# Storing half of three prepared operands out of seven, and rounding their high halves again when they are needed, in a fused attention and two-MoE kernel

## The chip, the cores and the metric

The kernel runs on one core of one Trainium2 chip. The metric is the device time of that core in microseconds; less is better. TensorE (PE) does the matrix products, VectorE (DVE), ScalarE (ACT) and GpSimd (POOL) the work between them, and SyncE (SP) issues every transfer. PEld is the load of weights into TensorE, DMA the sixteen transfer engines.

## The reference

Three layers follow each other on 2304 tokens:

```python
q_p, k_p = (phi(q_s), phi(k_s))          # random features, 32 heads
num = einsum(q_p, einsum(k_p, v)); den = einsum(q_p, sum(k_p))
x = (num / den), regrouped to [2304, 512]

logits = x @ w_gate                       # first MoE: 8 experts, all used
P = exp(logits - max); 8 times: P /= row sums, P /= column sums, P *= N/E
for e in range(8):
    h = maximum(x @ w1[e], 0)             # w1[e]: 512 x 1024
    out += P[:, e:e+1] * (h @ w2[e])      # w2[e]: 1024 x 512

h = maximum(maximum(x @ m1, x @ m2), x @ m3)   # second MoE, weights in float64
return h @ m_out
```

## The kernel before

Every operand of a product is split into a high part, rounded to the type that TensorE multiplies quickly, and a low part, the rest; a product is three matmuls (high by high, high by low, low by high: lines 406 to 408 and 808 to 810). The large products are done as seven products of half size instead of eight. For that the four blocks of a weight matrix are combined to seven operands, numbered 0 to 6: operands 0, 1 and 2 are blocks of the weight as it stands, 3 to 6 are sums and differences of blocks. A prepared operand is its high part and its low part side by side.

**Stages.** After attention (to about 145 us) the first MoE works on a third of the tokens at a time. *Stage 1* (about 145 to 690 us) takes the first third and runs through 32 slices of 256 hidden features, called subs. For each sub it loads w1 and w2 as they stand (512 KB each) into the tiles g, makes the sums on DVE or POOL, the high parts on ACT (L212) and the low parts on DVE or POOL (all those are recorded at L215), multiplies, and **stores all seven prepared operands** of w1 (`w1_store`) and of w2 (`prepare_w2`) in DRAM: 14 blocks of 128 KB for w1 and as many for w2, 1792 KB each. A sub is 42 matmuls of 384 columns and 36 of 512. *Phases 1 and 2* (about 690 to 1160 and to 1630 us) do the other two thirds: 16 units of two subs each, 168 matmuls of 384 columns a unit, and load the prepared operands instead of making them. w1's go into the one tile wa (256 KB a load, `before` in the loop over units), w2's into w2_0 to w2_6 (512 KB a load, in `second`). *Phases 3 to 5* are the second MoE, whose weights are prepared during phase 1 (`narrow`, `last_weights`) and loaded from lc1 and lc2.

**Order.** `Tasks` records each instruction with what it reads and writes and an estimated cost; `ordered` then plays a list schedule and writes out one fixed order for each engine. TensorE's own order is the program's; that of DVE, POOL, ACT and SP, and which of DVE and POOL takes a piece, follows from the costs, a transfer's bytes among them. Every engine then runs its list in order: an instruction that waits holds all behind it. `x_operands(1)` and `x_operands(2)` prepare the tokens of phases 1 and 2 (14 stores of 384 KB each, xc<-h) whenever the schedule has room in stage 1.

Of the kernel before, what the change touches and what calls it, by code (L numbers as in the profile page):

```python
# [8 lines left out]
F32 = mybir.dt.float32  # L9
# [145 lines left out]
def tile_performer__moe__max3(ctx, tc, kq_t, kq, v1, omega2, w_gate, w1, w2, m1, m2, m3, m_out, out):  # L155
# [7 lines left out]
    P = 128  # L163
# [60 lines left out]
    IN_B = {"w2_2", "w2_3", "w2_4", "w2_5", "w2_6", "b11", "b12", "b21", "b22", "t1", "t2", "t3", "t4", "pb", "ones"}  # L224
# [29 lines left out]
    def t_(k):  # L254
        return ts[k]
# [72 lines left out]
    def w1_store(s):  # L328
        dma(1792, lambda: wc1[s], lambda: ws[s % 2].bitcast(F32), all_w(s % 2), [("wc1", s)])
# [23 lines left out]
    def prepare_w2(s, late):  # L353
# [8 lines left out]
        for c, k in enumerate((h, l)):  # L362
            v = lambda k=k: t_(k).rearrange("p (k f) -> p k f", k=2).bitcast(F32)
            dma(256, lambda c=c: wc2[u][:, 0:2, c, sub], lambda v=v: v()[:, :, 0:256], [(k, 0), (k, 1)], [("wc2", u, sub, c)])
            dma(128, lambda c=c: wc2[u][:, 2, c, sub], lambda v=v: v()[:, 1, 256:], [(k, 1)], [("wc2", u, sub, 2 + c)])

        def rest():
# [5 lines left out]
            for c, k in enumerate(("w2_4", "w2_5")):  # L373
                dma(512, lambda c=c: wc2[u][:, 3:7, c, sub], lambda k=k: t_(k).rearrange("p (o f) -> p o f", o=4).bitcast(F32),
                    [(k, 0), (k, 1)], [("wc2", u, sub, 4 + c)])
# [128 lines left out]
    def retranspose(t):  # L504
# [7 lines left out]
        gi = g_next("st")  # L512
# [59 lines left out]
    def g_pieces():  # L572
        return [
            (lambda k=k, i=i: gs[k][:, i * 512 : i * 512 + Q], half(k, i)) for k in range(3) for i in range(2)
        ]
# [46 lines left out]
    def last_weights(item):  # L622
        n, m = item // 4, item % 4
        f0 = n * UF
        for at in range(2):
# [5 lines left out]
            narrow(lambda src=src: src, wide, at, 2, 3, at)  # L631
        if m < 3:
            add_all(left_operands(1, 3, 4, first_of(1)))
            dma(1792, lambda: lc1[3 * n + m], lambda: ws[1].bitcast(F32), all_w(1), [("lc1", 3 * n + m)])
        else:
# [4 lines left out]
            dma(1024, lambda: lc2[n].rearrange("p c f -> p (c f)"), lambda: flat()[:, 0:2048].bitcast(F32), ks[:8], [("lc2", n)])  # L640
# [40 lines left out]
    def program():  # L681
# [113 lines left out]
        def second(ph, u, j, d, n):  # L795
# [3 lines left out]
            if d == 0 and (ph == 1 or n):  # L799
                keys = [("wc2", u, sub, c) for sub in range(2) for c in range(6)]  # L800
# [559 lines left out]
```

## Time and profile before

| | us |
|---|---|
| median of 3 runs (lowest, highest) | 1948.44 (1946.2, 1950.5) |
| the profiled execution's own time | 1947.44 |
| span of its profile, first to last instruction | 1945.7 |

The page of the profile gives the busy share of each engine over the span: PE 97%, DVE 76%, POOL 52%, ACT 41%. 84.1% of the time of the sixteen DMA engines goes to the one queue that SP fills; 392.65 MB are read from DRAM and 177.26 MB written. The busy time of PE is modelled for pipelined matmuls, so the number of matmuls that a stretch completes tells more than its busy share. Such tables by stretch are called windows here.

### The profile page before, as it was taken

To read this page: it belongs to the slowest core of one execution; us is meant where nothing else is said; L and a number is where in the kernel's file an instruction comes from. 1 tells how busy PE (TensorE), PEld (TensorE's weight loads), DVE (VectorE), ACT (ScalarE), POOL (GpSimd) and SP (SyncE) were. 2 spreads that over 40 slices of the span, in tenths; PEclk is the share of its full clock that TensorE was granted. 3 is DMA by queue.
4 is the path that set the end of the run, shared out by engine and by line. 5 is a ranking of instruction groups with operands and counts; after the bars stand their busy time and mean duration, and the time that the engine had idled before them with its cause. 6 is when DMAs were issued, how large, how long until landed. Compare 5 with 4: busy or idle time off the path is not lost.

```text
span 1945.7 us, 33270 instructions
## 1 busy us (share of the span) xinstructions
PE 1881.6 (97%) x11521; PEld 1778.9 (91%) x11521; DVE 1482.3 (76%) x2676; ACT 796.9 (41%) x1805; POOL 1010.1 (52%) x933
## 2 busy tenths in 40 slices
PE   8997899899999999999999999999999999999998
PEld 6876788779999999999999998999999999989998
DVE  7874887778777766999989988999977767443435
ACT  7874345445444435333333333433433333232221
POOL 4532687335644416677777866677776444230000
PEclk9998999999999999999999999999999999999999
DMA  6655889979988899999898998988899889997673
GB/s 240 187 163 184 298 308 363 349 273 354 332 285 294 332 346 344 344 323 312 291 319 293 310 340 282 318 309 310 312 334 364 277 253 319 351 337 249 205 239 119
DMA packets 278759, 572.12 MB, mean 294 GB/s; under 512 B 26080, under 2 KB 125120, under 8 KB 272960
## 3 DMA queue, kind: packets, MB, share of 16 engines
q1 hardware_dynamic: 278592, 570.01, 84.1%
q8 instruction: 91, 1.49, 0.3%
q14 instruction: 76, 0.62, 0.1%
HBM read 392.65 MB, written 177.26 MB: 293 GB/s over the span
## 4 chain that ended last, share of the span: by engine, by line
PE 87%; DVE 6%; DMA 3%; ACT 2%; issue 1%; POOL 1%; SPq 0%; DVEq 0%; ACTq 0%
PE po L406 8%; PE po L408 8%; PE po L407 8%; PE ph L408 6%; PE ph L406 6%; PE ph L407 6%; PE ph L810 5%; PE ph L808 5%; PE ph L809 5%; PE ph L476 3%; PE ph L478 3%; PE ph L477 3%; PE small L810 3%; PE small L808 3%; PE small L809 3%; PE small L478 2%
## 5 line engine op out<-in xcount | busy, mean ns | idle before, releaser
L215 POOL TENSOR_TENSOR h<-b,h 128x384 fp32r<-128x384 f32 x149 | 164.6, 1112 | 177.5 <-ACT h L756 156.0
L406 PE MATMUL po<-x,wa 128*128 128x384 f32 x676 | 227.3, 336 | 4.0 <-DVE po L215 2.3
L407 PE MATMUL po<-x,wa 128*128 128x384 f32 x676 | 226.9, 336 | 0.0
L408 PE MATMUL po<-x,wa 128*128 128x384 f32 x676 | 226.8, 336 | 0.0
L406 PE MATMUL ph<-x,wa 128*128 128x384 f32 x588 | 199.6, 339 | 12.1 <-ACT wa L212 7.4
L408 PE MATMUL ph<-x,wa 128*128 128x384 f32 x588 | 199.7, 340 | 3.8 <-DVE wa L215 3.5
L810 PE MATMUL ph<-h,w 128*128 128x384 f32 x598 | 202.5, 339 | 0.0
L808 PE MATMUL ph<-h,w 128*128 128x384 f32 x598 | 202.3, 338 | 0.0
L809 PE MATMUL ph<-h,w 128*128 128x384 f32 x598 | 201.6, 337 | 0.0
L407 PE MATMUL ph<-x,wa 128*128 128x384 f32 x588 | 198.9, 338 | 0.0
L215 DVE TENSOR_TENSOR po<-po,u 128x384 f32<-128x384 f32 x230 | 129.0, 561 | 89.5 <-PE po L408 86.2
L215 DVE TENSOR_TENSOR acc<-ph,acc 128x384 f32<-128x384 f32 x280 | 154.0, 551 | 52.6 <-PE ph L810 51.6
L756 ACT CAST h<-b 128x384 fp32r<-128x384 f32 x192 | 98.8, 516 | 231.6 <-DVE b L771 207.5
L756 ACT CAST h<-t 128x384 fp32r<-128x384 f32 x256 | 129.2, 515 | 152.5 <-POOL t L215 104.0
L215 POOL TENSOR_TENSOR g<-g,g 128x256 f32<-128x256 f32 (+2 forms) x150 | 151.5, 1012 | 58.1 <-DVE g L617 23.3
L215 POOL TENSOR_TENSOR h<-t,h 128x384 fp32r<-128x384 f32 x126 | 137.4, 1091 | 85.0 <-ACT h L756 72.9
L413 ACT COPY u<-po 128x384 f32<-128x384 f32 x186 | 89.4, 482 | 182.1 <-PE po L408 178.6
L215 POOL TENSOR_TENSOR wb<-g,wb 128x512 fp32r<-128x512 f32 (+2 forms) x101 | 126.7, 1263 | 56.7 <-ACT wb L212 50.3
L413 ACT COPY u<-ph 128x384 f32<-128x384 f32 x183 | 88.0, 481 | 152.6 <-PE ph L408 151.2
L215 POOL TENSOR_TENSOR w<-g,w 128x512 fp32r<-128x512 f32 (+1 forms) x60 | 75.7, 1272 | 122.9 <-ACT w L212 50.7
L406 PEld LDWEIGHTS po<-x,wa 128*128 128x128 f32 x676 | 127.0, 188 | 6.8 <-DVE po L215 3.0
L476 PE MATMUL ph<-w,h 128*128 128x512 f32 x328 | 131.4, 401 | 0.0
(221 smaller groups left out, 5319.6 us busy)
## 6 DMA issues: line engine op xcount, KB each, us to landing
wa<-wc SPq DMA_DIRECT2D x441, 256.0 KB, 4.9
w<-wc SPq DMA_DIRECT2D x217, 512.0 KB, 5.5
g<-in_moe_w_dram SPq DMA_DIRECT2D x82, 512.0 KB, 6.1
wc<-w SPq DMA_DIRECT2D x64, 512.0 KB, 7.4
wc<-wa SPq DMA_DIRECT2D x16, 1792.0 KB, 9.0
wc<-wb SPq DMA_DIRECT2D x16, 1792.0 KB, 8.6
x<-xc SPq DMA_DIRECT2D x64, 384.0 KB, 7.4
wb<-lc SPq DMA_DIRECT2D x91, 256.0 KB, 4.6
```

Of the source, the lines that this page charges most:

```text
L215: (nc.gpsimd if on == "P" else nc.vector).tensor_tensor(out=out, in0=in0, in1=in1, op=op)
L406: nc.tensor.matmul(ps, w[:, 0, c], x[c][:, 0], start=c == 0 and not onto, stop=False, **given)
L407: nc.tensor.matmul(ps, w[:, 0, c], x[c][:, 1], start=False, stop=False, **given)
L408: nc.tensor.matmul(ps, w[:, 1, c], x[c][:, 0], start=False, stop=c == 1, **given)
L413: act(Q, lambda: nc.scalar.copy(t_(n), banks[b][:, :Q]), [b], [n])
L476: nc.tensor.matmul(ps, h[:, 0, c], t_(wh)[:, part], start=f == 0, stop=False)
L477: nc.tensor.matmul(ps, h[:, 0, c], t_(wl)[:, part], start=False, stop=False)
L478: nc.tensor.matmul(ps, h[:, 1, c], t_(wh)[:, part], start=False, stop=f == 1)
L756: act(Q, lambda: nc.scalar.copy(t_(h)[:, 0], t_(n)), [n], [(h, 0)])
L808: nc.tensor.matmul(ps, wv[:, 0, sub, d], h[:, 0], start=o == 0, stop=False)
L809: nc.tensor.matmul(ps, wv[:, 0, sub, d], h[:, 1], start=False, stop=False)
L810: nc.tensor.matmul(ps, wv[:, 1, sub, d], h[:, 0], start=False, stop=o == 1)
```

## The change

In stage 1 the high parts of operands 0, 1 and 2 are no longer stored. Their low parts go to new tensors wl1 and wl2, operands 3 to 6 go to wc1 and wc2 as before: 384 + 1024 KB a sub instead of 1792 KB, for w1 and for w2 alike. In phases 1 and 2 `load_w1` and `second` fetch the block of the weight itself for these three operands into one of six staging places of 128 KB (four quarters of g1, and the new tiles st0 and st1), and ACT rounds it into place (`round_high`); the low part is loaded beside it. The bytes loaded stay the same. A unit has 6 such operands of w1 (one raw load and one low load each) and 3 of w2 (two raw loads and one low load each): 33 transfers instead of 21, and 12 more copies of 256 columns on ACT. All prepared weights lie in DRAM as blocks, one operand behind the other, and no longer interleaved within a partition's row. Since g1 is the staging tile, the token copies after stage 1 use other g tiles, and `narrow` loads both of its pieces through g0.

```diff
-    wc1 = [dram.tile([P, 7, 2, 256], F32, name=f"wc1_{s}") for s in range(SUBS)]
-    wc2 = [dram.tile([P, 7, 2, 2, 256], F32, name=f"wc2_{u}") for u in range(UNITS)]
-    lc1 = [dram.tile([P, 7, 2, 256], F32, name=f"lc1_{a}") for a in range(9)]
-    lc2 = [dram.tile([P, 2, 1024], F32, name=f"lc2_{n}") for n in range(3)]
+    wl1 = [dram.tile([3, P, 256], F32, name=f"wl1_{s}") for s in range(SUBS)]
+    wc1 = [dram.tile([4, P, 2, 256], F32, name=f"wc1_{s}") for s in range(SUBS)]
+    wl2 = [dram.tile([3, P, 2, 256], F32, name=f"wl2_{u}") for u in range(UNITS)]
+    wc2 = [dram.tile([4, P, 2, 2, 256], F32, name=f"wc2_{u}") for u in range(UNITS)]
+    lc1 = [dram.tile([7, P, 2, 256], F32, name=f"lc1_{a}") for a in range(9)]
+    lc2 = [dram.tile([2, P, 1024], F32, name=f"lc2_{n}") for n in range(3)]
...
     def w1_store(s):
-        dma(1792, lambda: wc1[s], lambda: ws[s % 2].bitcast(F32), all_w(s % 2), [("wc1", s)])
+
+        kl, k = w_keys(s % 2, 0, 3)[1], w_keys(s % 2, 3, 7)
+        dma(384, lambda: wl1[s].rearrange("o p f -> p o f"), lambda: ws[s % 2][:, 0:3, 1].bitcast(F32), kl, [("wl1", s)])
+        dma(1024, lambda: wc1[s].rearrange("o p c f -> p o c f"), lambda: ws[s % 2][:, 3:7].bitcast(F32), k[0] + k[1], [("wc1", s)])
...
-        for c, k in enumerate((h, l)):
-            v = lambda k=k: t_(k).rearrange("p (k f) -> p k f", k=2).bitcast(F32)
-            dma(256, lambda c=c: wc2[u][:, 0:2, c, sub], lambda v=v: v()[:, :, 0:256], [(k, 0), (k, 1)], [("wc2", u, sub, c)])
-            dma(128, lambda c=c: wc2[u][:, 2, c, sub], lambda v=v: v()[:, 1, 256:], [(k, 1)], [("wc2", u, sub, 2 + c)])
+        v = lambda: t_(l).rearrange("p (k f) -> p k f", k=2).bitcast(F32)
+        dma(256, lambda: wl2[u][0:2, :, sub].rearrange("o p f -> p o f"), lambda: v()[:, :, 0:256], [(l, 0), (l, 1)], [("wl2", u, sub, 0)])
+        dma(128, lambda: wl2[u][2, :, sub], lambda: v()[:, 1, 256:], [(l, 1)], [("wl2", u, sub, 1)])
...
             if d == 0 and (ph == 1 or n):
-                keys = [("wc2", u, sub, c) for sub in range(2) for c in range(6)]
-                dma(512, lambda: t_(w).bitcast(F32), lambda: wc2[u][:, i].rearrange("p c s f -> p (c s f)"), keys, [(w, 0), (w, 1)])
+                keys = [("wl2" if i < 3 else "wc2", u, sub, c) for sub in range(2) for c in range(2)]
+                if i < 3:
+                    e, f0 = u // 2, u % 2 * 2 * UF
+                    for sub in range(2):
+                        high = lambda sub=sub: t_(w)[:, sub * 256 : (sub + 1) * 256]
+                        row = f0 + sub * UF + min(i, 1) * P
+                        round_high(high, lambda x: x, w2[e, row : row + P, slice(256, 512) if i == 2 else slice(0, 256)], [(w, 0)])
+                    dma(256, lambda: t_(w)[:, 512:].bitcast(F32), lambda: wl2[u][i].rearrange("p s f -> p (s f)"), keys, [(w, 1)])
+                else:
+                    dma(512, lambda: t_(w).bitcast(F32), lambda: wc2[u][i - 3].rearrange("p c s f -> p (c s f)"), keys, [(w, 0), (w, 1)])
...
+        stage = [(lambda q=q: gs[1][:, q * 256 : (q + 1) * 256], ("g1", q)) for q in range(4)]
+        stage += [(lambda k=k: t_(k), k) for k in ("st0", "st1")]
+
+        def round_high(out, shape, raw, keys):
+
+            stage.insert(0, stage.pop())
+            x, k = stage[0]
+            dma(128, lambda: shape(x()), lambda: raw, [], [k])
+            act(256, lambda: nc.scalar.copy(out(), x()), [k], keys)
+
+        def load_w1(s, i, kh, kl):
+            if i > 2:
+                dma(256, lambda: ws[0][:, i].bitcast(F32), lambda: wc1[s][i - 3], [("wc1", s)], kh + kl)
+                return
+            raw = w1_raw(s)[:, 2 * min(i, 1) : 2 * min(i, 1) + 2, P * (i // 2) : P * (i // 2 + 1)]
+            round_high(lambda: ws[0][:, i, 0], lambda x: x.rearrange("p (k f) -> p k f", k=2), raw, kh)
+            dma(128, lambda: ws[0][:, i, 1].bitcast(F32), lambda: wl1[s][i], [("wl1", s)], kl)
...
                         if ph == 1 or not first:
-                            dma(256, lambda: ws[0][:, i].bitcast(F32), lambda: wc1[s][:, i], [("wc1", s)], kh + kl)
+                            load_w1(s, i, kh, kl)
```

The first place that the prediction speaks of is SP's list in stage 1, from the store of sub 10's w1 operands on. Here wa and wb are the two tiles of prepared w1, w_0 to w_5 those of prepared w2, g the weights as loaded, b<-x_of and xc<-h the loads and stores of the tokens that x_operands prepares. Before:

```order
L218 DMA wc_10_106<-wa 128x3584
L218 DMA g_83<-in_moe_w_dram 128x2x512
L218 DMA b_2780<-x_of_87 128x384
L218 DMA xc_92<-h_2537 128x768
L218 DMA wc_5_133<-w_0_2535 128x2x256
L218 DMA wc_5_133<-w_0_2535 128x256
L218 DMA wc_5_133<-w_1_2536 128x2x256
L218 DMA wc_5_133<-w_1_2536 128x256
L218 DMA xc_92<-h_2541 128x768
L218 DMA xc_92<-h_2538 128x768
L218 DMA wc_4_132<-w_4_2776 128x4x256
```

Now:

```order
L220 DMA wl_10_106<-wa 128x3x256
L220 DMA g_83<-in_moe_w_dram 128x2x512
L220 DMA wc_4_180<-w_4_2823 128x4x256
L220 DMA wc_10_138<-wa 128x4x512
L220 DMA wc_4_180<-w_5_2824 128x4x256
L220 DMA wl_5_165<-w_1_2584 128x2x256
L220 DMA wl_5_165<-w_1_2584 128x256
L220 DMA wc_11_139<-wb 128x4x512
L220 DMA g_81<-in_moe_w_dram 128x4x256
L220 DMA wl_11_107<-wb 128x3x256
```

The stores of the high halves (w_0) are gone, and the token stores no longer stand here. Over the whole list, the 28 token stores xc<-h stood between the w1 stores of subs 1 and 13 before; now they stand between those of subs 1 and 21. Between the w1 stores of subs 5 and 16 there were 24, and there are 16.

The second place is SP's list in phase 1, where sub 17's weights are loaded (wa) and unit 8's (w_0, w_6, w_3). Before:

```order
L218 DMA w_2_2774<-wc_7_135 128x1024
L218 DMA wa<-wc_17_113 128x512 x2
L218 DMA w_0_2535<-wc_8_136 128x1024
L218 DMA wa<-wc_17_113 128x512 x2
L218 DMA w_6_2778<-wc_8_136 128x1024
L218 DMA wa<-wc_17_113 128x512 x2
L218 DMA w_3_2775<-wc_8_136 128x1024
L218 DMA wa<-wc_17_113 128x512
```

Now:

```order
L220 DMA w_2_2821<-wl_7_167 128x512
L220 DMA wa<-wl_17_113 128x256
L220 DMA g_82<-in_moe_w_dram 128x2x128
L220 DMA wa<-wc_17_145 128x512
L220 DMA g_82<-in_moe_w_dram 128x2x128
L220 DMA w_0_2583<-wl_8_168 128x512
L220 DMA g_82<-in_moe_w_dram 128x2x128
L220 DMA st_2838<-in_moe_w_dram 128x256
L220 DMA g_82<-in_moe_w_dram 128x256
L220 DMA wa<-wc_17_145 128x512
L220 DMA wa<-wl_17_113 128x256
```

The raw loads into the staging places (g_82 is g1, st) stand between the loads of the prepared weights.

The third place is ACT's list in the first half of a unit of phase 1, from the rounding of the first product of hidden features (h<-b) on. u are copies of products out of PSUM. Before:

```order
L756 CAST h_2537<-b_2779 128x384
L756 CAST h_2539<-b_2782 128x384
L756 CAST h_2540<-t_2783 128x384
L413 COPY u_2532<-po 128x384
L756 CAST h_2542<-t_2785 128x384
L413 COPY u_2533<-po 128x384
L413 COPY u_2534<-po 128x384
```

Now:

```order
L760 CAST h_2585<-b_2826 128x384
L760 CAST h_2587<-b_2829 128x384
L867 CAST wa<-g_82 128x256
L760 CAST h_2588<-t_2830 128x384
L417 COPY u_2580<-po 128x384
L867 CAST wa<-st_2839 128x256
L760 CAST h_2590<-t_2832 128x384
L417 COPY u_2581<-po 128x384
L417 COPY u_2582<-po 128x384
```

The roundings of the raw weights (L867) stand between the copies of PSUM and the casts of hidden features, and each waits for a raw load and for its place in wa or w.

## Rows read from the trace of the kernel before

**Rows 1.** The page, span and line 1 (busy, share, instructions of each engine).

```profile
span 1945.7 us, 33270 instructions
...
PE 1881.6 (97%) x11521; PEld 1778.9 (91%) x11521; DVE 1482.3 (76%) x2676; ACT 796.9 (41%) x1805; POOL 1010.1 (52%) x933
...
```

**Rows 2.** Windows: busy us (instructions) by engine, clock, DMA share, GB/s, by stage.

```profile
...
core 0: us, PE busy (x) PEld busy (x) DVE busy (x) ACT busy (x) POOL busy (x), PEclk, DMA share, GB/s
145.00:262.00 117.00, 93.58 (x517) 79.77 (x516) 86.73 (x177) 46.66 (x101) 61.80 (x62) 0.90 0.70 248
262.00:450.00 188.00, 173.88 (x821) 151.95 (x821) 147.52 (x253) 88.43 (x180) 101.77 (x98) 0.96 0.92 334
450.00:690.00 240.00, 240.00 (x1194) 216.61 (x1194) 193.16 (x324) 114.37 (x230) 115.16 (x122) 1.00 0.88 314
690.00:820.00 130.00, 129.93 (x732) 126.72 (x731) 96.40 (x158) 55.65 (x120) 69.12 (x63) 1.00 0.98 350
820.00:1150.00 330.00, 330.00 (x1891) 330.00 (x1891) 301.90 (x502) 118.41 (x246) 245.50 (x219) 1.00 0.90 311
...
```

**Rows 3.** Waits of PE, 262 to 450 us: total, times, longest.

```profile
engine line waited for: us in total, times, longest us
PE po L408 <- DVE wb L215: 6.5, 5, 2.8
PE ph L408 <- DVE wa L215: 3.5, 4, 1.4
PE ph L406 <- ACT wa L212: 2.2, 1, 2.2
PE po L406 <- ACT wb L212: 2.0, 2, 1.2
...
```

**Rows 4.** Timeline of DVE around the stall at 354 us: start, duration.

```profile
...
353.97 0.75 DVE L499 SCALAR_TENSOR_TENSOR acc<-ph,prob,acc 128x512 f32<-128x512 f32 x1 [0.31 <-PE ph L478]
354.63 0.94 DVE L215 TENSOR_TENSOR g<-g 128x256 f32<-128x256 f32 x1
355.50 1.48 DVE L215 TENSOR_TENSOR wb<-g,wb 128x512 fp32r<-128x512 f32 x1
...
```

**Rows 5.** Tile g, issue to landing, 262 to 450 and 450 to 690 us.

```profile
...
DMA to landing us min/median/max: 4.1/8.8/12.8
...
DMA to landing us min/median/max: 3.8/6.2/10.0
```

**Rows 6.** DMA packets and bytes, 262 to 450, 450 to 690, 820 to 1150 us.

```profile
...
DMA packets 36434, 62.72 MB, mean 334 GB/s; under 512 B 2127, under 2 KB 29388, under 8 KB 35020
...
DMA packets 44692, 75.47 MB, mean 314 GB/s; under 512 B 2349, under 2 KB 37688, under 8 KB 42681
...
DMA packets 42522, 102.68 MB, mean 311 GB/s; under 512 B 4290, under 2 KB 8423, under 8 KB 41725
...
```

**Rows 7.** DMA issues of the span: xcount, KB each, median us to landing.

```profile
...
wa<-wc SPq DMA_DIRECT2D x441, 256.0 KB, 4.9
w<-wc SPq DMA_DIRECT2D x217, 512.0 KB, 5.5
...
wc<-wa SPq DMA_DIRECT2D x16, 1792.0 KB, 9.0
...
xc<-h SPq DMA_DIRECT2D x28, 384.0 KB, 5.9
...
```

**Rows 8.** Tile wa, 820 to 1150 us: issue on SP, issue to landing.

```profile
...
L218 SPq DMA_DIRECT2D wa<-wc x159: 319/319/2702, 818.0 to 1149.0; - x159
...
DMA to landing us min/median/max: 2.7/4.9/10.8
```

**Rows 9.** Groups of ACT, 820 to 1150 us: busy, mean ns, idle before, releasers.

```profile
...
L756 ACT CAST h<-t 128x384 fp32r<-128x384 f32 x89 | 44.8, 515 | 62.1 <-POOL t L215 41.1 <-DVE t L215 12.2 <-PE ph L810 6.6
L756 ACT CAST h<-b 128x384 fp32r<-128x384 f32 x68 | 35.1, 516 | 82.1 <-DVE b L771 75.9 <-PE ph L810 3.6 <-PE small L810 2.5
...
L212 ACT CAST wb<-g 128x256 fp32r<-128x256 f32 x5 | 2.0, 406 | 0.0
```

More of the change, by code (lines that the diff above doesn't have):

```diff
@@ L373, in rest @@
             for c, k in enumerate(("w2_4", "w2_5")):
-                dma(512, lambda c=c: wc2[u][:, 3:7, c, sub], lambda k=k: t_(k).rearrange("p (o f) -> p o f", o=4).bitcast(F32),
-                    [(k, 0), (k, 1)], [("wc2", u, sub, 4 + c)])
+                dma(512, lambda c=c: wc2[u][:, :, c, sub].rearrange("o p f -> p o f"), lambda k=k: t_(k).rearrange("p (o f) -> p o f", o=4).bitcast(F32),
+                    [(k, 0), (k, 1)], [("wc2", u, sub, c)])
         if late:
@@ L511, in retranspose @@
         pe(4 * 110, run, acc_keys(t * DM, (t + 1) * DM), [b])
-        gi = g_next("st")
+        gi = g_next("s")
         act(DM, lambda: nc.scalar.copy(gs[gi][:, :DM], banks[b]), [b], whole(gi))
@@ L573, in g_pieces @@
         return [
-            (lambda k=k, i=i: gs[k][:, i * 512 : i * 512 + Q], half(k, i)) for k in range(3) for i in range(2)
+            (lambda k=k, i=i: gs[k][:, i * 512 : i * 512 + Q], half(k, i)) for k in (0, 2, 3) for i in range(2)
         ]
@@ L630, in last_weights @@
                 src, wide = m_out[f0 + P * at : f0 + P * (at + 1), :], lambda x: x
-            narrow(lambda src=src: src, wide, at, 2, 3, at)
+            narrow(lambda src=src: src, wide, 0, 2, 3, at)
         if m < 3:
             add_all(left_operands(1, 3, 4, first_of(1)))
-            dma(1792, lambda: lc1[3 * n + m], lambda: ws[1].bitcast(F32), all_w(1), [("lc1", 3 * n + m)])
+            dma(1792, lambda: lc1[3 * n + m].rearrange("o p c f -> p o c f"), lambda: ws[1].bitcast(F32), all_w(1), [("lc1", 3 * n + m)])
         else:
@@ L639, in last_weights @@
                         lambda k: ks[2 * k : 2 * k + 2], lambda k: ks[4 + 2 * k : 6 + 2 * k])
-            dma(1024, lambda: lc2[n].rearrange("p c f -> p (c f)"), lambda: flat()[:, 0:2048].bitcast(F32), ks[:8], [("lc2", n)])
+            dma(1024, lambda: lc2[n].rearrange("c p f -> p c f"), lambda: flat()[:, 0:2048].rearrange("p (c f) -> p c f", c=2).bitcast(F32), ks[:8], [("lc2", n)])
     def gate():
@@ L914, in before @@
                         if ph == 3 or a > 1:
-                            dma(256, lambda: ws[slot][:, i].bitcast(F32), lambda: lc1[mat][:, i], [("lc1", mat)], kh + kl)
+                            dma(256, lambda: ws[slot][:, i].bitcast(F32), lambda: lc1[mat][i], [("lc1", mat)], kh + kl)
                         if a == 0:
@@ L1300, in tile_performer__moe__max3 @@
         ts.update({("pb", j, k): b.tile([P, Q], F32, name=f"pb{j}{k}") for j in range(2) for k in range(2)})
+        ts.update({k: b.tile([P, 256], F32, name=k) for k in ("st0", "st1")})
         ts["ones"] = b.tile([P, P], F32, name="ones")
```

4 lines of the change are left out of this document (2 added, 2 removed).

## The prediction

> **What bounds the kernel now.** I read the page first: TensorE is busy 97% of a span of 1945.7 us [rows 1]. So a gain can only come from the few places where TensorE does not run at its own pace, and the next view must find them. The windows by stage do it by counts of matmuls [rows 2]. From 450 to 690 us, in the later part of stage 1, TensorE ends 1194 matmuls in 240 us, 4.975 per us, with a busy time equal to the window and clock 1.00: that is the stage's full pace. From 262 to 450 us the same mix of work gives 821 in 188 us. At full pace they would take 821 / 4.975 = 165.0 us, so **23.0 us are lost between 262 and 450 us**. From 145 to 262 us there is a loss too (517 matmuls, some of attention's among them), and from 690 to 1150 us there is practically none: busy 129.93 of 130 and 330.00 of 330.
>
> Who ends the waits in the losing stretch? TensorE's waits there name the prepared w1 operands, low parts from DVE and high parts from ACT: 6.5 + 3.5 + 2.2 + 2.0 = 14.2 us [rows 3]. The clock is 0.96 in this window against 1.00 in the next, and 0.04 of 188 us is 7.5 us; together 21.7 of the 23.0. So the clock's share goes with the waits and is not a second cause.
>
> Why are the operands late? DVE's timeline at the stall of 354 us shows the preparation of wb starting only at 354.63, behind an accumulation, with no gap in front [rows 4]. DVE itself is not fuller here than later: 147.52 of 188 us is 78%, and 193.16 of 240 is 80% where nothing is lost [rows 2]. What differs is the transfers. The raw weights (tile g) take a median of 8.8 us from issue to landing here, 12.8 at most, against 6.2 and 10.0 later [rows 5], and the DMA share is 0.92 at 334 GB/s against 0.88 at 314 [rows 2]. The stretch carries 62.72 MB [rows 6]: the stores of stage 1 and most of the 28 token stores of 384 KB (xc<-h) [rows 7].
>
> **The change part by part.**
>
> *Stores removed.* Six blocks of 128 KB a sub are not written, 0.786 MB. A sub is 78 matmuls, so the losing stretch holds 821 / 78 = 10.5 subs: 8.3 MB less. The new order of SP moves 8 token stores of 0.393 MB out of it, 3.1 MB more. Left are 62.72 - 8.3 - 3.1 = 51.3 MB; in 165 us that is 311 GB/s. It lies under the 314 GB/s at which the window from 450 to 690 us loses nothing, and that later window falls as well: 1194 / 78 = 15.3 subs save 12.0 of its 75.47 MB [rows 6] and it takes on the 3.1. So I expect the raw weights to land as they land later now (6.2 us), and the waits of [rows 3] to go. The planner has the smaller bytes too and puts DVE's pieces earlier, so the order doesn't hold what the transfers give. Not all of the 23.0 us will come back, since some stalls follow from the order of DVE and POOL; bounds are 0 (the waits name DVE and ACT, not a DMA) and 23. Since the nearest row, the next window, has no loss at the same DVE load, I take 20.
>
> *145 to 262 us.* DVE's list up to there is almost that of before, and the waits there belong to the gate. Nothing is taken; a gain of up to 5 us or a loss of as much stays in the range.
>
> *Loads in phases 1 and 2.* Bytes are unchanged. Packets are more: a raw w1 block comes in 512-byte runs (256) and its low part in 1 KB runs (128) where 128 runs of 2 KB came; a w2 operand in 256 + 128 instead of 128. That is 256 more for each of 9 operands, 2304 a unit. TensorE's pace is 1891 / 330 = 5.73 per us, a unit of 168 matmuls lasts 29.3 us, so 79 packets more per us on top of 42522 / 330 = 129 [rows 6]. Is a packet costly? Stage 1 moves 44692 / 240 = 186 packets per us at 314 GB/s with a share of 0.88, phase 1 moves 129 at 311 GB/s with 0.90 [rows 2, 6]. More packets at equal bytes do not raise the share, so a packet costs nothing that these rows show; at the other end, if bytes cost nothing, each is worth 0.90 / 129 and the share would go to 1.45, which stage 1's own row excludes (186 would need 1.30). 208 per us is close to stage 1's 186, so I take no cost from 820 us on. From 690 to 820 us the share is 0.98 already and the loads have no room: I take 1 us there, with 0 and 6 as bounds (6 would be a share of 1.05 over 130 us).
>
> The Trainium skill speaks against this part: its page "DMA: Bandwidth & Descriptors", section "Rules for kernel authors", says to coalesce many small transfers into one large one, and asks for 1 MiB or more for full bandwidth. Here 256 KB loads become two of 128 KB, and 1792 KB stores are cut. The trace does not bear it out as long as transfers overlap: wa's loads of 256 KB run beside others at 311 GB/s and TensorE never waits for one between 820 and 1150 us. By the rule the phases would lose, by the rows nothing; the rule's case is priced below as a rival.
>
> *SP.* An issue takes 0.32 us when nothing holds it [rows 8]. 33 a unit are 10.6 us of 29.3 instead of 6.7: hidden, as SP spends the rest waiting for places. Without that cover it would be 3.9 us a unit.
>
> *ACT.* 12 casts of 256 columns a unit at 0.406 us [rows 9] are 4.9 us a unit, on top of 118.41 / 330 x 29.3 = 10.5 [rows 2]: 15.4 of 29.3. Hidden in time. In order they stand ahead of the copies u, which DVE needs and TensorE's banks after it. A cast waits for its raw load and for its place. Six staging places serve twelve loads a unit, so a load is issued about half a unit, 14.7 us, before its cast, and the longest landing of wa in this stretch is 10.8 us, the median 4.9 [rows 8]. I take no wait.
>
> *g tiles.* `narrow` through one g tile makes the second MoE's weights later; they are needed only after 1630 us. Nothing. *Blocks* for lc1 and lc2 keep the loads at 2 and 4 KB a run: nothing.
>
> **Sum** against the profiled execution's own time of 1947.44: 1947.4 - 20 + 1 = 1928.4. The median of the runs is 1.0 us above that execution, so I say 1929 us.
>
> **The rivals.**
>
> *The stalls are the order's, not the transfers'.* For it: the waits name DVE and ACT, and DVE has no gap before the late piece [rows 3, 4]. Against it: the next window, as full on DVE, has none. Then only a few waits go, some 4 us: 1944.
>
> *The small transfers fill the DMA in phases 1 and 2.* Price: share times 940 us beyond 1.0. If a packet cost 0.0020 of share per packet and us, the share would be 0.90 + 79 x 0.0020 = 1.06, 0.06 x 940 = 56 us: 1947 + 56 - 20 = 1983. It decides from 1.02 on (20 / 940), 0.0015 per packet. The Trainium skill's rule on small transfers, cited above, leads here. Against it stand stage 1's 186 packets.
>
> *ACT is held by a late raw load* (the other side): place, the casts in front of the copies u of a unit. For it: ACT already waits 82.1 + 62.1 us in 330 for DVE and POOL [rows 9], so it may free staging places late, which SP's list then waits for, with every load behind it. Against it: 14.7 us ahead against 10.8. TensorE has no spare time in these phases, so each us lost a unit is 31 us in all: 1 us gives 1959; it decides from 20 / 31 = 0.65 us a unit.
>
> **How the numbers follow.** The forecast (1919 to 1938) gets 0.61, a gain beyond it (early stalls too) 0.05, the order's stalls 0.15, the full DMA 0.06, the held ACT 0.13. 0.2% of 1948 is 3.9 us, about what a measurement of this kernel can tell from no change: faster is the first two and half of the third, 0.73; same is the other half and a mild form of the last, 0.09; slower 0.18. The range from 1915 to 1952 leaves out the deep gain and the dear forms of the last two, some 0.18.
>
> **What would show it.** Right: in the changed profile the stretch from 262 us on has 4.9 matmuls per us or more, no waits for wa or wb beyond 3 us, tile g landing near 6 us, 25.2 MB less written (32 subs); phases 1 and 2 keep 5.73 per us. Wrong: the same waits at a lower DMA share (the order's); a DMA share of 1.0 and TensorE waiting for wa or w<-wl in phase 1 (transfers); ACT waiting for g<-in_moe_w or st, and TensorE behind u (ACT).

## The result, and the profile after

| | before | after |
|---|---|---|
| median of 4 runs each, us (lowest, highest) | 1947.32 (1945.45, 1950.5) | 1915.3 (1912.39, 1918.66) |
| the profiled execution's own time, us | 1947.44 | 1912.39 |
| span of its profile, us | 1945.7 | 1910.6 |

The ratio is 0.9834 with an interval of 0.982 to 0.9849: 32 us less, where 19 were forecast (-20 + 1). The direction was right. The size was too small, and the reason given for the largest term was wrong, as the experiments show.

The page of the changed kernel (busy us, share and instructions of each engine, then bytes), beside [rows 1]:

```profile
span 1910.6 us, 34524 instructions
...
PE 1865.7 (98%) x11521; PEld 1771.2 (93%) x11521; DVE 1456.9 (76%) x2639; ACT 916.1 (48%) x2180; POOL 1043.3 (55%) x970
...
HBM read 392.65 MB, written 152.09 MB: 285 GB/s over the span
```

It writes 25.2 MB less and reads as much. ACT has 375 instructions and 119 us of busy time more. Its windows, with columns as in [rows 2] and bounds shifted so that each holds about the same matmuls:

```profile
145.00:256.00 111.00, 90.49 (x509) 79.02 (x505) 81.54 (x177) 47.31 (x101) 61.48 (x62) 0.91 0.65 220
256.00:420.00 164.00, 164.00 (x817) 148.04 (x816) 141.82 (x226) 87.26 (x178) 118.89 (x122) 1.00 0.93 319
420.00:661.00 241.00, 241.00 (x1199) 217.49 (x1198) 197.00 (x328) 117.37 (x235) 119.21 (x118) 1.00 0.82 279
661.00:791.00 130.00, 128.58 (x726) 125.52 (x725) 93.19 (x155) 71.24 (x169) 67.55 (x63) 1.00 0.97 330
791.00:1122.00 331.00, 329.89 (x1887) 329.25 (x1886) 282.85 (x482) 158.27 (x375) 232.59 (x213) 1.00 0.91 300
```

The losing stretch now runs at full pace: 817 matmuls in 164 us are 4.98 per us, at clock 1.00, and the waits of TensorE between 256 and 420 us are an empty list where [rows 3] had 14.2 us. But look at the share of the DMA: **0.93, not lower than the 0.92 before**. Fewer bytes (the 52.35 MB below) in less time left the engines as full as they were. (This share adds up the times of all packets, so it can pass 1.) The raw weights do land earlier, 6.6 us at the median against 8.8 [rows 5]. DMA packets of 256 to 420, 420 to 661 and 791 to 1122 us, as in [rows 6]:

```profile
DMA packets 40216, 52.35 MB, mean 319 GB/s; under 512 B 1848, under 2 KB 29633, under 8 KB 40202
...
DMA packets 53051, 67.16 MB, mean 279 GB/s; under 512 B 2382, under 2 KB 39640, under 8 KB 53033
...
DMA packets 73476, 99.41 MB, mean 300 GB/s; under 512 B 6395, under 2 KB 45361, under 8 KB 73445
```

Tile g of 256 to 420 us, from issue to landing:

```profile
DMA to landing us min/median/max: 3.6/6.6/9.2
```

In stage 1 every sign that the prediction had named for being right has come true: the pace, the empty list of waits, the landing near 6 us, the 25.2 MB. They could not tell its reason from its rival's, since the change alters the lists as well as the bytes; the experiments can.

**Where the time came from, by the same instructions.** TensorE's list is the program's and the same in every kernel here (11521 matmuls in each trace), so matmul number n is the same instruction in all of them. The next table is worked out from the traces: the us between the starts of the same two matmuls, cut at the columns' times in the kernel before (the first column from the first matmul on). Each row is one profiled execution; the kernels with the lists of before (fewer_bytes_same_lists and blocks_only) differ from it by up to 1.6 us in the first column, 1.1 from 145 to 262 and around 1150, and at most 0.3 in the others outside of 262 to 450. Kernels below the second row are the experiments.

```
                        0-145 145-262 262-450 450-690 690-820 820-1150 1150-1200 1200-1740 1740-1900
before                  141.0   116.9   188.0   240.1   129.9    330.2      49.9     540.0     160.0
after                   139.6   110.8   165.0   240.1   131.3    331.8      45.6     540.0     156.7
order_alone             140.4   112.9   166.6   240.1   129.6    330.2      50.0     540.0     159.8
bytes_alone             141.1   125.2   185.5   240.1   133.5    330.2      51.2     540.1     156.9
fewer_bytes_same_lists  140.4   115.8   185.0   240.1   129.9    330.2      50.9     540.0     160.3
tokens_late             140.1   111.6   164.9   249.5   131.0    330.2      48.6     540.1     160.6
before_wire             140.3   111.3   175.4   240.1   132.1    330.2      48.7     543.2     158.3
w1_only                 141.1   111.8   170.0   240.1   132.2    330.2      48.6     540.1     159.1
w2_only                 143.8   114.5   173.5   240.3   130.8    331.2      48.8     540.0     158.1
blocks_only             139.4   116.4   188.3   240.1   129.9    330.2      51.0     540.1     159.8
narrow_one              143.7   114.9   188.9   240.1   129.6    330.2      47.9     540.0     160.0
cast_twice              141.6   111.9   165.0   240.1   129.6    330.8      48.1     542.4     157.3
g_tiles                 140.5   114.9   188.6   240.1   132.4    330.2      46.2     540.1     160.1
g_tiles_order           142.7   112.8   166.7   240.1   129.6    330.2      45.9     540.7     159.5
reduce_cost             139.8   106.7   168.6   240.1   130.4    330.7      45.6     540.1     156.4
reduce_wire             140.8   106.4   167.7   240.1   138.9    332.0      51.4     557.1     154.2
```

After against before: -23.0 from 262 to 450 us, -6.1 from 145 to 262, -4.3 around 1150, -3.3 from 1740 on, +3.0 from 690 to 1150, -1.4 ahead of 145 (a column in which kernels with the same lists differ by as much). Together it is -35.1, the difference of the two spans.

### The profile page after: what moved, and what is told of

Its sections match the earlier page's. It is cut to its first block, busy times and chain, and to the rows that moved or that the text cites. A ratio compares the mean times of both kernels' runs of the same rounds, so it can differ in the third digit from the quotient of the medians.

```text
span 1910.6 us, 34524 instructions
## 1 busy us (share of the span) xinstructions
PE 1865.7 (98%) x11521; PEld 1771.2 (93%) x11521; DVE 1456.9 (76%) x2639; ACT 916.1 (48%) x2180; POOL 1043.3 (55%) x970
## 4 chain that ended last, share of the span: by engine, by line
PE 91%; DVE 4%; ACT 2%; DMA 2%; issue 1%; SPq 0%; POOL 0%; DVEq 0%; ACTq 0%
PE po L410 9%; PE po L411 9%; PE po L412 9%; PE ph L410 6%; PE ph L412 6%; PE ph L411 6%; PE ph L822 5%; PE ph L820 5%; PE ph L821 5%; PE ph L480 4%; PE ph L482 4%; PE ph L481 4%; PE small L822 3%; PE small L820 3%; PE small L821 3%; PE small L482 2%
## 5 line engine op out<-in xcount | busy, mean ns | idle before, releaser
L217 POOL TENSOR_TENSOR g<-g,g 128x256 f32<-128x256 f32 (+2 forms) x164 | 163.4, 998 | 87.8 <-DVE g L217 32.8
L217 DVE TENSOR_TENSOR acc<-ph,acc 128x384 f32<-128x384 f32 x280 | 154.2, 551 | 49.5 <-PE ph L822 48.2
L217 POOL TENSOR_TENSOR h<-t,h 128x384 fp32r<-128x384 f32 x131 | 142.1, 1089 | 89.9 <-ACT h L760 78.9
L217 POOL TENSOR_TENSOR wb<-g,wb 128x512 fp32r<-128x512 f32 (+2 forms) x108 | 132.7, 1235 | 51.2 <-ACT wb L214 43.9
L217 POOL TENSOR_TENSOR t<-b,b 128x384 f32<-128x384 f32 x106 | 111.8, 1071 | 34.9 <-DVE b L775 31.6
```

The source lines that it names most:

```text
L217: (nc.gpsimd if on == "P" else nc.vector).tensor_tensor(out=out, in0=in0, in1=in1, op=op)
```

## The experiments

Theory A, the prediction's, is that fewer bytes let the raw weights land earlier. Theory B is that the list changes: the planner is told the bytes of each transfer (`kb * 1024 / 340` ns on one wire) and writes out another fixed order. The first four kernels tell these apart.

**order_alone**: the kernel before, with all its transfers; only the bytes that the planner is told of the stores are the change's.

```diff
-        dma(1792, lambda: wc1[s], lambda: ws[s % 2].bitcast(F32), all_w(s % 2), [("wc1", s)])
+        dma(1408, lambda: wc1[s], lambda: ws[s % 2].bitcast(F32), all_w(s % 2), [("wc1", s)])
...
-            dma(256, lambda c=c: wc2[u][:, 0:2, c, sub], lambda v=v: v()[:, :, 0:256], [(k, 0), (k, 1)], [("wc2", u, sub, c)])
+            dma(256 * c, lambda c=c: wc2[u][:, 0:2, c, sub], lambda v=v: v()[:, :, 0:256], [(k, 0), (k, 1)], [("wc2", u, sub, c)])
...
```

> The kernel before with all its stores, but the planner is told the new, smaller bytes for them, so that the instruction lists are those of a kernel with fewer stores while the transfers are not fewer. If the bytes are what matters, the stretch of stage 1 that lost 23.0 us stays overfull and most of the loss stays: 1938 to 1950 us. If the order of the lists does it (token stores spread out, pieces of DVE placed earlier), most of the gain of the whole change comes without it: 1915 to 1925 us.

Measured: 1922.04 us, ratio 0.9872 [0.9856, 0.9888]. Windows and tile g's landing of 262 to 450 us:

```profile
262.00:450.00 188.00, 187.12 (x928) 168.12 (x928) 164.90 (x262) 101.18 (x208) 137.69 (x137) 1.00 1.03 375
...
DMA to landing us min/median/max: 4.4/7.0/10.8
```

928 matmuls in the 188 us where 821 were, at 375 GB/s and a share above 1.0. Not a byte less is stored in all, and the stretch takes 166.6 us: 21.4 of the 23.0 us come from the lists alone. Nor has the list merely moved bytes out of the stretch: between the same two matmuls 61.4 MB are moved here and 62.7 before.

**bytes_alone**: the changed kernel, its planner told the old bytes of these stores.

```diff
-        dma(384, lambda: wl1[s].rearrange("o p f -> p o f"), lambda: ws[s % 2][:, 0:3, 1].bitcast(F32), kl, [("wl1", s)])
+        dma(768, lambda: wl1[s].rearrange("o p f -> p o f"), lambda: ws[s % 2][:, 0:3, 1].bitcast(F32), kl, [("wl1", s)])
...
```

(and the like for the two stores to wl2.)

> The changed kernel with its fewer stores, but the planner is told the old bytes of the w1 and w2 stores. If the bytes matter, the stretch from 262 us on runs at full pace although the lists are made for slower transfers: 1912 to 1925 us. If the order does it, the late pieces and the dense token stores come back, and with them most of the 23 us: 1932 to 1942 us.

Measured: 1952.83 us, 1.0035 [1.0022, 1.0047]. **All the change's transfers with a list planned for the old ones are slower than before.** Window and waits of TensorE, 262 to 450 us:

```profile
262.00:450.00 188.00, 174.87 (x830) 153.88 (x829) 144.89 (x247) 87.46 (x179) 98.10 (x96) 0.97 0.82 282
```

```profile
PE ph L412 <- DVE wa L217: 5.2, 1, 5.2
PE po L412 <- DVE wb L217: 4.8, 6, 1.4
PE po L410 <- ACT wb L214: 2.5, 2, 1.2
```

The share fell to 0.82 and waits of the same kind stayed. Between the same two matmuls this kernel moves 52.2 MB, as the changed kernel does, and takes 185.5 us where that takes 165.0. The total is above the range that was given for the lists: the stretches from 145 and from 690 us lose 8.3 and 3.6 us against before as well.

**fewer_bytes_same_lists**: the lists and costs of the kernel before, and fewer bytes. In the traces TensorE, DVE, ACT and POOL run the same instructions in the same order as before; SP's list lacks 128 stores of w2's operands.

```diff
-        dma(1792, lambda: wc1[s], lambda: ws[s % 2].bitcast(F32), all_w(s % 2), [("wc1", s)])
+        dma(1792, lambda: wc1[s][:, 3:7], lambda: ws[s % 2][:, 3:7].bitcast(F32), all_w(s % 2), [("wc1", s)])
...
-            dma(128, lambda c=c: wc2[u][:, 2, c, sub], lambda v=v: v()[:, 1, 256:], [(k, 1)], [("wc2", u, sub, 2 + c)])
+            add("S", 128 * 1024 / 340, lambda e: None, [(k, 1)], [("wc2", u, sub, 2 + c)])
...
```

> The kernel before with its own instruction lists and planner costs, but operands 0 to 2 are not stored at all (a third to a half of the bytes of the stage's stores gone, 1.57 MB a sub), and phases 1 and 2 load operands 3 to 5 a second time in their place, so that loads are as before; the products of phases 1 and 2 are made of other weights. If the transfers' bytes hold stage 1 up, its loss of 23 us must go, since twice as many bytes are taken away as by the change: 1915 to 1927 us. If the fixed order of DVE's list holds it up, the list is still the old one and the loss stays: 1938 to 1950 us.

Measured: 1946.33 us, 0.9999 [0.999, 1.0009]. Window, waits and landing of tile g, 262 to 450 us:

```profile
262.00:450.00 188.00, 174.40 (x836) 152.76 (x835) 151.07 (x256) 91.13 (x185) 104.98 (x101) 0.98 0.70 249
...
PE po L408 <- DVE wb L215: 6.8, 5, 2.7
PE ph L408 <- DVE wa L215: 3.5, 4, 1.4
...
DMA to landing us min/median/max: 3.5/5.3/8.9
```

With a quarter of the traffic gone the raw weights land at 5.3 us and the two waits for DVE of [rows 3] (6.5 and 3.5) are still there. DVE's timeline at the same stall as [rows 4] shows why (start, duration, idle before):

```profile
347.74 0.75 DVE L499 SCALAR_TENSOR_TENSOR acc<-small,prob,acc 128x512 f32<-128x512 f32 x1 [0.77 <-PE small L478]
...
349.32 0.56 DVE L453 SCALAR_TENSOR_TENSOR h<-ph,h 128x384 fp32r<-128x384 f32 x1 [0.37 <-ACT h L452]
350.19 0.75 DVE L499 SCALAR_TENSOR_TENSOR acc<-ph,prob,acc 128x512 f32<-128x512 f32 x1 [0.31 <-PE ph L478]
350.86 0.94 DVE L215 TENSOR_TENSOR g<-g 128x256 f32<-128x256 f32 x1
351.72 1.48 DVE L215 TENSOR_TENSOR wb<-g,wb 128x512 fp32r<-128x512 f32 x1
```

The raw loads of w1 and w2 issued at 338.04 and 339.17 us had landed at 342.72 and 346.48. Between then and 350.19 DVE was idle three times, 0.77, 0.37 and 0.31 us, waiting for TensorE's products and ACT, but its list has the accumulation of 350.19 in front of the first piece of the weights. The kernel before shows the same at the stall of [rows 4]. Its w1 load for this wb is issued at 341.83 us (tile g, 341.9 to 342 us):

```profile
L218 SPq DMA_DIRECT2D g<-in_moe_w_dram x1: 384/384/384, 341.8 to 341.8; - x1
...
DMA to landing us min/median/max: 5.3/5.3/5.3
```

So w1 had landed at 347.17, 7.5 us ahead of the piece at 354.63. ACT's list does the like: it rounds wb's first pieces only at 352.96, after idling 0.52, 1.62 and 0.90 us for other work of DVE and TensorE. And SP's list issues this load 11.9 us ahead of the first matmul that needs it, where order_alone issues it 20.8 and the changed kernel 25.5 us ahead. The transfers have a small part: before, the sub whose matmuls start at 302.9 us has its w1 only at 302.17 and waits 2.2 us; here it has it 9.3 us ahead of the same matmul and still waits 1.2.

In the changed kernel the same accumulation stands at 340.31, and the pieces of wb are long done:

```profile
327.47 0.68 DVE L217 TENSOR_TENSOR wb<-g,wb 128x512 fp32r<-128x512 f32 x1
328.07 0.74 DVE L503 SCALAR_TENSOR_TENSOR acc<-ph,prob,acc 128x512 f32<-128x512 f32 x1
328.73 0.41 DVE L217 TENSOR_TENSOR g<-g,g 128x256 f32<-128x256 f32 x1
329.06 0.41 DVE L217 TENSOR_TENSOR wb<-g,wb 128x256 fp32r<-128x256 f32 x1
...
340.31 0.75 DVE L503 SCALAR_TENSOR_TENSOR acc<-ph,prob,acc 128x512 f32<-128x512 f32 x1 [0.17 <-PE ph L482]
340.97 0.77 DVE L217 TENSOR_TENSOR wa<-g,wa 128x512 fp32r<-128x512 f32 x1
```

Counted in the traces up to the same matmul (353.94 us in the kernel before): 42 pieces of wb written before and in fewer_bytes_same_lists, 48 in order_alone and after, which have also begun the next wa.

**tokens_late**: the kernel before; the token loads of phases 1 and 2 may not be planned ahead of the end of subs 7 and 15.

```diff
-                dma(192, pieces[p][0], src(i, j), given(i, j), pieces[p][1])
...
+                    tasks.add("S", 192 * 1024 / 340, lambda e, o=pieces[p][0], x=src(i, j): fetch(o(), x()), [], pieces[p][1], gate_x[0])
...
+            if s in (8, 16):
+                gate_x[0] = tasks.last
```

> The kernel before with all its stores; only the loads of the tokens for phases 1 and 2 may not be planned before the end of subs 7 and 15, so the 28 token stores leave the crowded stretch or spread out of it. If the loss is an overload of the transfers in that stretch, 10 to 20 us come back without any change of the weights: 1927 to 1937 us. If the loss is the preparation chain's own (DVE, ACT, POOL), the time stays within 5 us of 1947.

Measured: 1927.28 us, 0.99 [0.988, 0.992]. Windows 262 to 450 and 450 to 690 us:

```profile
262.00:450.00 188.00, 185.57 (x914) 166.77 (x913) 157.20 (x256) 96.93 (x196) 110.94 (x109) 0.99 0.94 339
450.00:690.00 240.00, 236.97 (x1169) 213.20 (x1168) 181.26 (x309) 112.16 (x225) 125.21 (x130) 0.99 0.94 338
```

Where the tokens no longer stand, the loss is gone (164.9 us); where they went, 9.4 us are lost. Both windows move as much per us, and so did the losing stretch before (334). So the loss goes with the token work in the plan; alone this run, which fell into the range given for the bytes, doesn't tell the bytes from the list.

**before_wire**: the kernel before, the planner's wire taken as 420 instead of 340.

```diff
-        return add("S", kb * 1024 / 340, lambda e: fetch(out(), in_()), r, w)
+        return add("S", kb * 1024 / 420, lambda e: fetch(out(), in_()), r, w)
```

> The kernel before with every transfer as it was; only the rate that the planner counts on for the queue of transfers is raised from 340 to 420 bytes per ns. By the order theory the planner then expects the raw weights earlier and puts DVE's preparation between the accumulations instead of behind the last one, as in the changed kernel: the 23 us come back with no byte less, 1915 to 1928 us. By the bytes theory nothing changes, or DVE now waits for loads that its list expects too early: 1945 to 1965 us.

Measured: 1931.65 us, 0.992 [0.9907, 0.9934]. Window and waits of TensorE, 262 to 450 us:

```profile
262.00:450.00 188.00, 180.65 (x885) 161.06 (x884) 157.66 (x246) 93.56 (x196) 128.54 (x127) 0.99 0.99 361
...
PE po L406 <- ACT u L413: 4.9, 2, 4.1
PE po L406 <- DVE po L215: 1.6, 1, 1.6
```

One figure of the planner takes 0.8% off with no byte less; half of the stretch's loss goes and other waits, behind ACT's copies, come. The time lies in neither of the two ranges.

**w1_only and w2_only**: the change for w1's operands alone, and for w2's alone (the other keeps its stores and loads, in blocks).

```diff
-        dma(384, lambda: wl1[s].rearrange("o p f -> p o f"), lambda: ws[s % 2][:, 0:3, 1].bitcast(F32), kl, [("wl1", s)])
-        dma(1024, lambda: wc1[s].rearrange("o p c f -> p o c f"), lambda: ws[s % 2][:, 3:7].bitcast(F32), k[0] + k[1], [("wc1", s)])
+        dma(1792, lambda: wc1[s].rearrange("o p c f -> p o c f"), lambda: ws[s % 2].bitcast(F32), all_w(s % 2), [("wc1", s)])
```

(that is w2_only's store; w1_only has the like for w2.)

> Half of the change: the high parts of w1's three operands alone are not stored and are rounded again; w2's seven are stored whole. By the bytes theory the saving in the crowded stretch is half (4.1 MB of 62.7), the demand there is then 55.4 MB in 165 us, 336 GB/s, still above the 314 at which nothing is lost, so less than half of the 23 us comes back: 1930 to 1938 us. If any lightening is enough since the order shifts with it, it is near the whole change: 1915 to 1922.

> The other half: the high parts of w2's three operands alone are not stored. The same bytes as the w1 half, so by the bytes theory the same 1930 to 1938 us. If it is the removed wait of the stores of w2's high tiles that counts (they hold w2_0 and w2_2 while stored), this half gives nearly all: 1915 to 1922, and the w1 half little.

Measured: 1924.48 us, 0.9878 [0.9863, 0.9894], and 1929.57, 0.9897 [0.9881, 0.9914]. Each half alone takes most of the loss of 262 to 450 us (18.0 and 14.5 of 23.0), so they don't add up. The w1 half lies between the two ranges and the w2 half just below that of the bytes, so neither expectation was met; w2's half gives less than w1's, so the stores that held w2_0 and w2_2 are not what counts.

**cast_twice**: the changed kernel, each of ACT's new roundings done twice.

```diff
             act(256, lambda: nc.scalar.copy(out(), x()), [k], keys)
+            act(256, lambda: nc.scalar.copy(out(), x()), [k], keys)
```

> The changed kernel with each rounding of a raw block done twice on ACT, some 375 casts of 0.4 us more; results do not change. In phase 1 the changed kernel is 3.0 us slower than before between the same matmuls. If that is ACT's doing (casts in front of the copies out of PSUM), doubling them adds another 3 us or more in phase 1 and as much in phase 2: 1919 to 1930 us. If it is the DMA's, it stays at 1913 to 1918.

Measured: 1916.95 us, 0.9835 [0.9821, 0.985]. Groups of ACT, 797 to 1128 us (L868 is the second rounding):

```profile
L868 ACT CAST wa<-g 128x256 fp32r<-128x256 f32 x45 | 18.3, 407 | 1.4
L867 ACT CAST wa<-g 128x256 fp32r<-128x256 f32 x45 | 18.3, 407 | 31.3 <-PE ph L411 16.2 <-PE po L411 12.1 <-DMA w<-wc 2.3
...
L867 ACT CAST w<-g 128x256 fp32r<-128x256 f32 x44 | 17.8, 405 | 9.6 <-DMA g<-in_moe_w_dram 9.6
```

As many again cost 1.6 us at the median, not to be told apart by the intervals, and 690 to 1150 us even takes 2.7 us less. From 1200 to 1740 us it takes 2.4 more, of which 1.4 are two waits of TensorE for u behind ACT. In phase 1 ACT is covered; in phase 2 nearly.

**blocks_only, narrow_one and g_tiles**: the kernel before with, in turn, the block layout; `narrow` through one g tile (the first edit of the second fence); all the change's edits of g tiles (all three of that fence).

```diff
-    wc1 = [dram.tile([P, 7, 2, 256], F32, name=f"wc1_{s}") for s in range(SUBS)]
+    wc1 = [dram.tile([7, P, 2, 256], F32, name=f"wc1_{s}") for s in range(SUBS)]
...
```

```diff
-            narrow(lambda src=src: src, wide, at, 2, 3, at)
+            narrow(lambda src=src: src, wide, 0, 2, 3, at)
...
-        gi = g_next("st")
+        gi = g_next("s")
...
-            (lambda k=k, i=i: gs[k][:, i * 512 : i * 512 + Q], half(k, i)) for k in range(3) for i in range(2)
+            (lambda k=k, i=i: gs[k][:, i * 512 : i * 512 + Q], half(k, i)) for k in (0, 2, 3) for i in range(2)
```

> The kernel before with the prepared weights laid out in blocks, all seven operands stored and loaded. If the layout matters (the 3.3 us won in phases 4 and 5, where the loads of lc1 and lc2 are the only thing that changed), this gains 2 to 5 us; if that gain is a shift of the order, or noise of one profile, the time stays at 1947 within 2 us, or rises by a little because the stores of w1 come in 2 KB runs instead of 14 KB.

> The kernel before with the second MoE's weights narrowed through one g tile instead of two, the side edit of the change. If the 4.3 us won at the start of phase 2 come from the narrowing pieces on DVE that stood there and now stand elsewhere, this kernel wins 3 to 5 us against before: 1942 to 1945. If they come from the loads of weights there, it stays at 1947.

> The kernel before with the changed kernel's use of the g tiles alone (tokens of phases 3 to 5 through g0, g2 and g3, narrowing through g0, the transposed tokens through the other ring); stores, loads and planner figures as before. If the 4.3 us won at the start of phase 2 and the 3.3 us won in phases 4 and 5 come from where these side pieces now stand in the lists, this kernel wins 4 to 8 us: 1940 to 1944 us. If they come from the raw loads, 1945 to 1949 us, with stage 1 as before in either case.

Measured: 1946.91 us, 1.0001 [0.9988, 1.0014]; 1941.88, 0.9978 [0.9964, 0.9993]; 1945.05, 0.9988 [0.9978, 0.9997]. The blocks do nothing. The g tiles give 3.7 us around 1150 and lose 2.5 from 690 to 820. TensorE's one wait of 1140 to 1200 us, before and in g_tiles:

```profile
PE ph L406 <- DVE po L215: 4.7, 1, 4.7
...
PE ph L406 <- DVE po L215: 2.5, 1, 2.5
```

narrow_one's runs spread from 1939.29 to 1947.33 us and its profiled one took 1946.46, so its row shows 2.0 us less around 1150 and not where its median of 5.9 us less comes from.

**g_tiles_order**: order_alone and the g tile edits together, so nearly all that the change does to the lists of stage 1 and of 1150 us, with every byte stored and no raw load in the phases.

> The kernel before with all its stores and loads, the planner told the new bytes of the stores, and the g tiles as in the changed kernel: every list effect of the change without one byte or raw load of it. If the whole gain is one of the lists, this reaches 1913 to 1919 us; if the raw loads and smaller stores bring the last part, it stays at 1920 to 1924 us as with the planner's figures alone.

Measured: 1918.96 us, 0.9849 [0.9834, 0.9863]: 29.2 us below its runs of before (1948.15), of the 32, without what the change is about. The intervals of the two ratios overlap. By the table the change then takes 2.0, 1.7 and 2.8 us less from 145, 262 and 1740 us on, and 3.3 more from 690 to 1150; another 3.1 less stand ahead of 145, where nothing differs that the change is about.

**reduce_cost and reduce_wire**: the changed kernel, told that a partition_all_reduce takes 14000 ns of POOL instead of 3000; then the wire of 420 as well.

```diff
-        add("P", 3000, lambda e: nc.gpsimd.partition_all_reduce(mx[:, 1:2], mx[:, 0:1], P, bass.bass_isa.ReduceOp.max), ["mx0"], ["mx1"])
+        add("P", 14000, lambda e: nc.gpsimd.partition_all_reduce(mx[:, 1:2], mx[:, 0:1], P, bass.bass_isa.ReduceOp.max), ["mx0"], ["mx1"])
```

> The changed kernel, with the planner told that GpSimd's reduction over partitions in the gate keeps it for 14 us instead of 3 (in the trace POOL shows 6 us without work before it and 7 us after). If the wait of 9.2 us near 176 us, and its size of 5.4 before the change, is set by what the planner puts behind that reduction on POOL, it goes and the time is 1904 to 1911 us. If the wait is for the loads of sub 2's weights, it stays: 1913 to 1918 us.

> The changed kernel with both planner figures corrected: 14 us for the reduction and 420 bytes per ns for the queue. Stage 1 after 262 us has nothing left to win in the changed kernel, so the rate should add nothing there to what the reduction gives: 1904 to 1912 us; a planner that now counts on transfers faster than they are in phases 1 and 2 could cost 2 to 10 us.

Measured: 1913.38 us, 0.9828 [0.9815, 0.9841], which can't be told from the change's 0.9834; and 1942.22, 0.9967 [0.9955, 0.9978]. Both lie above their ranges. The first takes 4.1 us off the stretch from 145 us, where the longest wait for wa falls from 9.0 to 1.7, and gives 3.6 back in the next. The second loses 17.1 us between 1200 and 1740 us and 7.6 from 690 us. Its waits for u from 1150 to 1650 us, of which the changed kernel has 0.6 us, make up part of that, and the clock is 0.99 from 1200 to 1650 us (1.00 in reduce_cost):

```profile
PE ph L410 <- ACT u L417: 7.2, 5, 3.9
PE ph L410 <- DVE po L217: 5.4, 1, 5.4
```

## Why the prediction was off

**The step that failed** is the term of -20 from 262 to 450 us: "So I expect the raw weights to land as they land later now (6.2 us), and the waits of [rows 3] to go." The bytes came as reckoned (51.3 MB forecast, 52.2 measured between the same two matmuls), they land at 6.6 us and the waits are gone, yet the one is not the cause of the other. fewer_bytes_same_lists lands them at 5.3 us and keeps 20 of the 23 us lost; order_alone stores everything and loses 1.6. That -20 came near the -23.0 measured is luck: with lists planned for the old bytes the transfers' part is 2.5 to 3 us (bytes_alone, fewer_bytes_same_lists). What led there was "What differs is the transfers": a share of 0.92 against 0.88 beside a stretch that loses time was a coincidence, as 375 GB/s at 1.03 with 0.7 us of waits shows. [rows 4] pointed at the answer, a late piece with no gap in front of it behind an accumulation, and the prediction read it as lateness of the data; the landing of that load, 7.5 us earlier, was in the same trace. The sentence on the planner's smaller bytes was in the text, as a help to the transfers, when it was nearly the whole.

Why the list of before puts the pieces there can be worked out from the program, which is argued and not measured. `ordered` sends all transfers over one wire and makes data ready 3500 ns after the wire:

```python
wire = max(wire, start) + cost
free[e], end = start + 60, wire + 3500
```

At 340 bytes per ns a sub's raw loads and stores (1024 + 3584 KB) take 13.9 us of this wire, and 24 token stores in 11 subs 2.5 us more (the token loads left out): 16.4 us, where a sub lasts 78 / 4.975 = 15.7. The wire is overbooked in the plan, raw weights arrive late in it, and DVE's pieces are put late. With 768 KB less and 16 token stores it is 11.6 + 1.7 = 13.3. The chip moved 375 GB/s there when asked to. The planner's own backlog ahead of 512 KB transfers (how long one would wait for the wire in the plan; the largest mean over some four subs, computed by the program, no measurement) ranks most kernels as the stage table does:

```
                backlog in the plan, about, us   lost 262-450 us (over 165.0)
before                   11                            23.0
bytes_alone              11                            20.5
w2_only                   9                             8.5
w1_only                   7                             5.0
order_alone               5                             1.6
after                     5                             0.0
tokens_late               9, in later subs             -0.1, and 9.4 from 450 to 690
before_wire               4                            10.4, other waits (ACT u)
```

before_wire doesn't fit: there the waits are for ACT's copies.

**145 to 262 us, 0 forecast, -6.1 measured.** Mostly the list: order_alone -4.0, bytes_alone +8.3, fewer_bytes_same_lists -1.1. The prediction held that DVE's list is almost that of before there, and did not look at the others. TensorE's waits before, 145 to 262 us, then in the changed kernel, 145 to 256 us:

```profile
PE small L666 <- DVE cs L661: 5.7, 2, 3.9
PE ph L406 <- ACT wa L212: 5.2, 1, 5.2
PE ph L666 <- DVE cs L661: 3.1, 3, 1.3
...
PE ph L412 <- DVE wa L217: 9.0, 1, 9.0
PE small L670 <- DVE cs L665: 3.6, 1, 3.6
...
PE ph L670 <- DVE cs L665: 1.0, 1, 1.0
```

The gate's waits (cs) shrank from 8.8 to 4.6 us (order_alone keeps 8.3, so its 4.0 us came elsewhere), and the wait for wa, already the longest of the kernel before, grew from 5.2 to 9.0. The changed kernel's POOL timeline shows what stands beside it:

```profile
163.48 1.71 POOL L217 TENSOR_TENSOR w<-g,w 128x512 fp32r<-128x512 f32 x1 [11.51 <-ACT w L214]
171.29 0.38 POOL L656 PARTITION_ALL_REDUCE mx<-mx  x1 [6.10 <-issue]
178.65 2.48 POOL L217 TENSOR_TENSOR w<-g,w 128x512 fp32r<-128x512 f32 x2 [6.98 <-issue]
```

**690 to 820 us, +1 forecast, +1.4 measured; 820 to 1150, 0 and +1.6.** Sizes right, and the reason of the +1 not shown: g_tiles and before_wire, without a raw load, take 132.4 and 132.1 from 690 to 820. cast_twice takes 129.6 and 330.8 there, so neither is a cost of ACT; what costs the 3 us was not settled.

**SP, ACT, packets: nothing, and at most those 3 us it was.** The share in phase 1 went from 0.90 to 0.91 at 73476 / 331 = 222 packets per us against 129 (208 were forecast), where the packet rival was priced at 1.06. The Trainium skill's rule cited in the prediction ("DMA: Bandwidth & Descriptors", "Rules for kernel authors") found no price here beyond the 3 us that stay unexplained: loads of 128 KB overlapped. The ACT rival needed a late raw load: ACT's wait for the loads into g is 13.3 us of 331 (and 5.4 for those into st), and TensorE's pace is 5.70 per us against 5.73. Groups of ACT, 791 to 1122 us, as in [rows 9]:

```profile
L867 ACT CAST w<-g 128x256 fp32r<-128x256 f32 x45 | 18.1, 404 | 13.3 <-DMA g<-in_moe_w_dram 13.3
L867 ACT CAST wa<-g 128x256 fp32r<-128x256 f32 x44 | 17.9, 407 | 43.1 <-PE ph L411 19.0 <-issue 16.7 <-PE po L411 3.1
```

**g tiles: nothing forecast, -4.3 measured** around 1150 us. g_tiles alone gives 46.2 us there and order_alone 50.0, so the edits suffice; bytes_alone has them too and takes 51.2, so this again is what the list makes of them. **1740 to 1900 us, nothing forecast, -3.3**: of it some 1.6 are TensorE's waits for token loads (`x<-xc` 3.2 before, 2.3 after, and 0.7 for b) and the rest goes with the granted clock (0.98 against 0.99 over 165 us). bytes_alone (156.9) and cast_twice (157.3) have it, and order_alone, blocks_only and g_tiles do not; but before_wire, with the old transfers, takes 158.3 and reduce_wire 154.2, so the transfers are not shown to be the cause. It stays open.

**The rival "the stalls are the order's"** had the mechanism, at 0.15, and the wrong time. It took the lists as given (1944, and with the lists held fixed 1946.33 was measured); but the change does alter them, by way of the planner's figures.

## What to carry to other kernels

Where a planner writes fixed lists, a change of bytes acts first through the figures that the planner is given: before crediting the transfers, run the old transfers with the new figures, and the new ones with the old. A late instruction with no gap in front of it may be late by its place in the list: see when its data landed, here 7.5 us earlier, before the transfers are blamed. A fuller DMA beside a slow stretch proves nothing until a run with fewer bytes and the same lists is faster there.

## What the runs showed of the hardware

The sixteen engines carried 375 GB/s over 188 us in order_alone, while TensorE ran at clock 1.00 with 0.7 us of waits; 334 GB/s before was no ceiling. A partition_all_reduce shows 0.38 us on POOL, with 6.10 us ahead of it and 6.98 behind it for which the trace names no releaser; that its reduction keeps POOL so long is a reading of these gaps, and telling the planner so moved 4.1 us out of that stretch, of which the next took 3.6 back.
